# A fused block-sparse attention and feed-forward kernel: the second of four batches moves from dense masked attention to gathered key blocks

## The chip, the cores and the metric

The kernel runs on one core of a Trainium2 chip. The metric is the device time of one execution in microseconds (us). Matmuls run on TensorE (PE in the profile; PEld is its weight load), elementwise work on VectorE (DVE), ScalarE (ACT) and GpSimd (POOL). SyncE (SP) issues most of the DMA transfers; POOL issues those that cast or gather by an index. Each engine works through its own instructions in order.

## The reference

What is computed is BigBird-like attention (4 batches, 8 heads, 768 tokens, head size 64), whose output goes through a feed-forward layer with a squared ReLU. Tokens form 24 blocks of 32. A query block sees itself and its two neighbours, the first and the last block, and three blocks drawn for it; the first and the last query block see everything.

```python
mask = np.abs(blk_i - blk_j) <= 1
mask = mask | (blk_i == 0) | (blk_j == 0) | (blk_i == 23) | (blk_j == 23)
for qb in range(24):
    for kb in sampled_blocks[qb]:                      # 3 per query block
        mask[qb*32:(qb+1)*32, kb*32:(kb+1)*32] = True
attn = softmax(where(mask, q @ k.T / 8, -1e9)) @ v      # per batch and head
x = attn.transpose(0, 2, 1, 3).reshape(3072, 512)
out = square(maximum(x @ moe_w_in, 0)) @ moe_w_out      # 512 -> 2048 -> 512
```

## The kernel before

**Two kinds of attention.** Heads are handled in pairs: a batch has four units u (u = 0 to 3 is batch 0, 4 to 7 batch 1, and so on). Batches below the constant `SB` (before: 2) are *dense*. For each unit and each 256 queries, `scores` multiplies the queries with two 128-key chunks at a time; `exps` (line 360, ACT) takes the exponential of 128 x 1024 numbers; then the forbidden ones have to go. That is done in one of two ways. With `add` true, `scores` adds a large negative mask on TensorE (two further pairs of matmuls of `oh` and `R2`, before the exponential). With `add` false, `masks` (line 367, DVE) multiplies the exponentials by a 0/1 mask; batch-wide mask tiles for this are made once by `mask_tile` on TensorE and evacuated by `mask_evac`. `values` or `values_full` multiplies with V, and `normalize` divides by the sum.

Batches from `SB` on are *gathered*. Their queries are taken in six *visits* of two groups g of 64 queries each. A group needs 12 blocks of 32 keys at most: a window of four, the first and the last block, and 2 x 3 drawn ones. `k_gather` copies the drawn blocks of K inside SBUF (on DVE or POOL, with block numbers held in registers). V is written out to DRAM by `v_store` (`rows`), and read back by `v_window` (SP, fixed addresses) and `v_gather` (line 579, an indirect DMA from POOL with the index tile `idx`, or plain DMAs from SP with block numbers in registers). `s_scores`, `s_exps` (line 623), `s_masks` (line 630) and `s_values` (line 653) then work on 384 keys for a group and not on 768, except for the group g = 0, which is the first and the last query block. Loads of Q and K of such a batch are in pieces of 512 bytes (line 151), of a dense one in pieces of 1536 bytes (line 149). Its output is stored in another order, too.

**The block table.** `table_load`, `table_places`, `table_slots`, `table_spread`, `table_rows` and `table_masks` make from `sampled_blocks` the index tile, the masks `MKS` of the gathered batches, and the row `tab`, from which engines read block numbers into registers (`blocks_of`, line 561: a TENSOR_LOAD in the queue of DVE, POOL or SP). `table_slots` is one task of some twenty small DVE instructions; `table_rows` reads all block numbers that any engine wants, one group after the other.

**The feed-forward layer.** The tokens form 12 tiles of 256. For each, `hidden` has 16 parts of 8 matmuls, `relu` and `square` follow on ACT, DVE or POOL, and `output` has 8 parts of 8 matmuls. TensorE alternates between the attention of one batch and the feed-forward tiles of an earlier one. The weights are loaded as eight pieces by POOL (`w_load`). `loads_gate` makes SP wait for pieces 6 and 7 before it issues the loads of batch 1 and later ones.

**The order.** Nothing is scheduled at run time. Every piece of work is a numbered task, and the string `PROGRAM` lists all tasks in one order, each with the letter of its engine (P, V, A, G, S) and, for a task that takes PSUM, the place (X0 to X3). An engine's instructions stand in the order of its words. The four PSUM places and all SBUF buffers are handed on in this order, so a late task holds up those behind it on its engine and those that need its buffer.

```python
MASKED = ((256, 512), (512, 768), (0, 256))     # mask tiles that are made
attend(a, us[0] < HP and a[1] == 0)             # add the mask on TensorE: batch 0, first 256 queries
```

## Time and profile before

| | |
|---|---|
| median of 3 runs | 255.62 us (254.7 to 257.25) |
| the profiled execution | 258.88 us, span of its trace 257.1 us |
| granted TensorE clock | 1.00 |
| PE / PEld busy | 243.1 / 182.1 us |
| ACT / DVE / POOL busy | 183.6 / 171.3 / 98.8 us |
| DMA moved | 47.08 MB |

The span runs from the first to the last instruction of the trace. "Busy" is the time in which an engine had at least one instruction running; a matmul's row includes a tail in which the next one is already in. A row of groups reads: line, engine, operation, tiles written and read, shapes, count, then busy time, mean ns of one, and the idle time ahead of them with what ended it. A timeline row reads: start, length, engine, line, operation, tiles, shapes, count, and in brackets the idle time ahead of it.

### The profile page before, as it was taken

To read this page: it belongs to the slowest core of one execution; us is meant where nothing else is said; L and a number is where in the kernel's file an instruction comes from. 1 tells how busy PE (TensorE), PEld (TensorE's weight loads), DVE (VectorE), ACT (ScalarE), POOL (GpSimd) and SP (SyncE) were. 2 spreads that over 40 slices of the span, in tenths; PEclk is the share of its full clock that TensorE was granted. 3 is DMA by queue.
4 is the path that set the end of the run, shared out by engine and by line. 5 is a ranking of instruction groups with operands and counts; after the bars stand their busy time and mean duration, and the time that the engine had idled before them with its cause. 6 is when DMAs were issued, how large, how long until landed. Compare 5 with 4: busy or idle time off the path is not lost.

```text
span 257.1 us, 12061 instructions
## 1 busy us (share of the span) xinstructions
PE 243.1 (95%) x5265; PEld 182.1 (71%) x5265; DVE 171.3 (67%) x408; ACT 183.6 (71%) x217; POOL 98.8 (38%) x178
## 2 busy tenths in 40 slices
PE   7888999999999997998998999999999999999993
PEld 4667879678874677975864867866875677767683
DVE  7778988899889995969916756657536725730301
ACT  3899999998999797846783975675965286623640
POOL 3183247003316026198556314264357620412100
PEclk9999999999999999999999999999999999999999
DMA  6999989999999996999699779998474923044022
GB/s 200 374 250 207 206 205 155 270 202 252 250 281 179 197 202 153 340 229 154 188 243 202 194 174 167 251 214 199 129 206 95 189 40 60 5 121 148 23 86 83
DMA packets 64692, 47.08 MB, mean 183 GB/s; under 512 B 31567, under 2 KB 60624, under 8 KB 64640
## 3 DMA queue, kind: packets, MB, share of 16 engines
q1 hardware_dynamic: 58512, 37.82, 64.7%
q0 software_dynamic: 5440, 8.05, 16.8%
q8 instruction: 41, 0.67, 1.1%
q10 hardware_dynamic: 688, 0.46, 0.6%
q14 instruction: 11, 0.09, 0.1%
HBM read 35.51 MB, written 7.91 MB: 169 GB/s over the span
## 4 chain that ended last, share of the span: by engine, by line
PE 53%; DVE 5%; DVEq 1%; issue 1%; ACT 1%; ACTq 0%
PE X L203 49%; PE X L653 4%; DVE VB L123 1%; ACT pT L623 1%; DVEq L561 1%; DVE MKS L123 1%; DVE pT L630 1%; DVE r L709 0%; DVE KG L599 0%; DVE qc L123 0%; DVE XS L413 0%; DVE KG L593 0%; DVE XS L662 0%; DVEq L599 0%; DVE rs L410 0%
## 5 line engine op out<-in xcount | busy, mean ns | idle before, releaser
L203 PE MATMUL X<-xT,w_in_sb 64*128 64x256 bf16 x1536 | 100.8, 269 | 2.8 <-issue 1.5
L203 PE MATMUL X<-w_out_sb,g 64*128 64x512 bf16 (+3 forms) x960 | 95.2, 334 | 0.1
L203 PEld LDWEIGHTS <-w_in_sb 64*128 64x128 bf16 x1536 | 74.6, 94 | 16.0 <-issue 5.4
L360 ACT ACTIVATE pT<-X 128x1024 bf16<-128x1024 f32 x72 | 70.6, 1030 | 7.6 <-PE X L203 6.8
L623 ACT ACTIVATE pT<-X 128x768 bf16<-128x768 f32 (+1 forms) x56 | 41.6, 766 | 26.5 <-PE X L203 23.9
L203 PEld LDWEIGHTS <-g 64*128 64x128 bf16 x960 | 40.3, 94 | 26.3 <-PE X L203 0.4
L720 POOL TENSOR_TENSOR g<-r 128x1024 bf16<-128x1024 f32 (+1 forms) x20 | 31.6, 1587 | 64.4 <-ACT r L707 47.2
L707 ACT ACTIVATE r<-X 128x1024 f32<-128x1024 f32 x28 | 29.8, 1068 | 20.6 <-PE X L203 20.5
L709 DVE TENSOR_SCALAR r<-X 128x1024 f32<-128x1024 f32 x20 | 24.5, 1224 | 26.7 <-PE X L203 13.7
L367 DVE TENSOR_TENSOR pT<-pT,VG 128x1024 bf16<-128x1024 bf16 x60 | 40.9, 715 | 0.2
L718 ACT ACTIVATE g<-r 128x1024 bf16<-128x1024 f32 (+1 forms) x40 | 35.2, 899 | 2.7 <-DVE r L709 2.5
L203 PE MATMUL X<-QKT 64*128 64x256 bf16 (+1 forms) x384 | 31.6, 250 | 3.3 <-DVE XS L413 1.3
L630 DVE TENSOR_TENSOR pT<-pT,MKS 128x768 bf16<-128x768 bf16 (+1 forms) x48 | 27.6, 607 | 10.7 <-ACT pT L623 10.5
L203 PEld LDWEIGHTS <-QKT 64*128 64x128 bf16 x384 | 16.7, 95 | 9.5 <-issue 4.1
L579 POOL DMA_INDIRECT VG<-rows,idx x19 | 20.2, 1061 | 4.4 <-issue 2.6
L203 PEld LDWEIGHTS <-pT 64*128 64x128 bf16 x768 | 16.0, 94 | 1.9
L203 PE MATMUL X<-VB,pT 64*128 64x65 bf16 x768 | 17.1, 190 | 0.0
L203 PEld LDWEIGHTS <-KG 64*128 64x128 bf16 x528 | 13.8, 95 | 4.5 <-issue 0.2
L659 DVE RECIPROCAL ss<-X 128x8 f32<-128x8 f32 x12 | 2.5, 206 | 19.5 <-PE X L653 17.3
L653 PEld LDWEIGHTS <-pT 128*64 128x64 bf16 x624 | 11.9, 111 | 4.9 <-issue 3.7
L203 PE MATMUL X<-QKT,KG 64*128 64x64 bf16 x528 | 15.3, 190 | 0.1
L123 POOL CAST VB<-vs 128x768 bf16<-128x768 f32 x9 | 7.8, 869 | 16.5 <-DMA vs<-in_v_dram 16.4
(107 smaller groups left out, 210.3 us busy)
## 6 DMA issues: line engine op xcount, KB each, us to landing
vs<-in_v_dram SPq DMA_DIRECT2D x14, 384.0 KB
ks<-in_k_dram SPq DMA_DIRECT2D x13, 384.0 KB
qs<-in_q_dram SPq DMA_DIRECT2D x12, 384.0 KB
out_dram<-ys SPq DMA_DIRECT2D x9, 512.0 KB
VG<-rows SPq DMA_DIRECT2D x20, 132.0 KB
w_in_sb<-in_moe_w_in_dram POOLq DMA_DIRECT2D x4, 512.0 KB, 8.6
w_out_sb<-in_moe_w_out_dram POOLq DMA_DIRECT2D x4, 512.0 KB, 9.9
rows<-VB SPq DMA_DIRECT2D x2, 792.0 KB
```

What stands on the lines that cost most here:

```text
L123: (V if e == "DVE" else G).tensor_copy(out=out, in_=in_)
L203: last = nc.tensor.matmul(out(r ^ crossed), lhsT(r ^ crossed, rows), rhs(r ^ crossed, rows), skip_group_check=True, **kw)
L360: A.activation(out=pT[:, :, 0:n], in_=stile.pop(a)[:, :, 0:n], func=AF.Exp, scale=scale)
L367: V.tensor_tensor(out=pT, in0=pT, in1=m[:, None].broadcast_to([P, 2, len(cs), w]), op=AOP.mult)
L579: G.indirect_dma_start(out=to[0:RS * HB], out_offset=None, in_=pairs, in_offset=bass.IndirectOffsetOnAxis(ap=idx[0:RS * HB, g - 1:g], axis=0))
L623: A.activation(out=pT[:, :, 0:n], in_=stile.pop((u, v, gs))[:, :, 0:n], func=AF.Exp, scale=scale)
L630: V.tensor_tensor(out=pT, in0=pT, in1=m[:, None].broadcast_to([P, 2, n]), op=AOP.mult)
L653: nc.tensor.matmul(po[i * D:(i + 1) * D, h, a * VW:(a + 1) * VW], pts[g][:, h, c * D:(c + 1) * D], val, start=a == 0 and c == 0, stop=c == ...
L707: A.activation(out=to, in_=src, func=AF.Relu)
L709: V.tensor_scalar(out=to, in0=src, scalar1=0.0, scalar2=None, op0=AOP.max)
L718: A.activation(out=g, in_=r, func=AF.Square)
L720: (G if e == "POOL" else V).tensor_mul(out=g, in0=r, in1=r)
```

## The change

- `SB` becomes 1: batch 1 is gathered too. It drops 36 `scores`, `exps` and `masks`, its `values` and `normalize`; it gains a `v_store`, six visits, 11 `k_gather` and 11 `v_gather`, and its Q and K loads and its stores take the forms of the gathered batches.
- `MASKED` becomes empty, and `attend` adds the mask on TensorE for all of batch 0. No mask tile is made, and no `masks` task is left.
- `table_slots` is cut into `table_ids`, `table_dup`, `table_near`, `table_drawn` and `table_low`; its scratch moves from two `r` buffers to the two `ys` buffers, so `table_places` waits for `cast_v` of units 2 and 3, and one memset goes from DVE to POOL. The reading of block numbers becomes six tasks of its own, groups 1 to 3 and groups 4 to 11 for each of POOL, DVE and SP.
- `PROGRAM` is a new list. In it the first tasks are nearly the old ones; the eight weight pieces are issued by POOL in the order 1, 2, 0, 7, 6, 4, 3, 5 (before: 1, 2, 0, 3, 7, 6, 4, 5), the table is made from about the tenth hidden part on, and the visits of batch 1 begin after 36 hidden and 8 output parts, while the tiles of batch 0 are in work. POOL takes 31 of the `v_gather` (before 19), 15 `k_gather` (10), 30 `square` (20), 21 `cast_qk` (14); DVE 18 `k_gather` (12), 24 `relu` (20), 15 `cast_qk` (21). On SP the last store of the last tile is its largest part (256 KB).

```diff
-    SB, VR, KG_BUFS, VG_BUFS = 2, D + 2, 2, 3
+    SB, VR, KG_BUFS, VG_BUFS = 1, D + 2, 2, 3
...
-    MASKED = ((256, 512), (512, 768), (0, 256))
+    MASKED = ()
...
+    def table_scratch():
+        tmp = [YS[b_.at] for b_ in tb["tmp"]]
...
     def table_places(e):
...
-    def table_slots(e):
-        tmp = RT[tb["tmp"][0].at]
...
+        low[0] = table_scratch()[-1]
+        G.memset(low[0], 0.0)
+
+    def table_ids(e):
         V.tensor_copy(out=tab..., in_=sb_r...)
-        V.memset(low[0], 0.0)
         V.tensor_copy(out=ids[:, 6:SL], in_=sb_g...)
+        V.tensor_scalar(out=half, in0=lane, ...)
+        V.tensor_tensor(out=lane, in0=lane, in1=half, op=AOP.add)
+
+    def table_dup(e):        # is_equal, scalar_tensor_tensor, tensor_reduce, tensor_scalar
+    def table_near(e):       # subtract, is_ge, is_le
+    def table_drawn(e):      # is_equal, tensor_reduce, max, edges, mult by dup
+    def table_low(e):        # eight copies into low[0]
...
     def table_rows(e):
         V.tensor_scalar(out=idx, ...)
-        load_blocks("POOL")
-        load_blocks("DVE")
-        load_blocks("SP")
...
-    def load_blocks(e):
-        for g in wanted[e]:
+    def load_blocks(g0, g1, e):
+        for g in [g_ for g_ in wanted[e] if g0 <= g_ < g1]:
             if g not in held_at[e]:
                 held_at[e][g] = blocks_of(g, ENGINE[e])
...
-    p = T_(table_places)
-    tmp = tb["tmp"] = [Buf("r"), Buf("r")]
-    tb["slots"] = T_(table_slots, deps=[t, p], get=tmp)
+    tmp = tb["tmp"] = [Buf("ys"), Buf("ys")]
+    p = T_(table_places, get=tmp)
+    i_ = tb["ids"] = T_(table_ids, deps=[t, p])
+    for e_ in ("POOL", "DVE", "SP"):
+        T_(load_blocks, 0, 4, deps=[i_])
+        T_(load_blocks, 4, nb, deps=[i_])
+    d_ = T_(table_dup, deps=[i_])
+    n_ = T_(table_near, deps=[i_])
+    w_ = T_(table_drawn, deps=[d_, n_])
+    l_ = T_(table_low, deps=[w_])
...
+        if us[0] == 0:
+            p.deps += cv[2] + cv[3]
...
-            attend(a, us[0] < HP and a[1] == 0)
+            attend(a, True)
...
     PROGRAM = """
-        A29 G35 P4/3 V32 P30/0 P12/2 P14/3 P9/1 P5/1 V31 P33/1 V111 P36/3 ...
+        A36 P4/0 P37/1 P12/2 P14/3 G42 P9/0 P5/2 V39 V38 P40/3 P43/0 P0/2 ...
```

## The prediction

> **What bounds the kernel now.** I read the page first, then the stretches of the span between points where the kind of work changes, then single rows for prices.

> ```profile
> span 257.1 us, 12061 instructions
> PE 243.1 (95%) x5265; PEld 182.1 (71%) x5265; DVE 171.3 (67%) x408; ACT 183.6 (71%) x217; POOL 98.8 (38%) x178
> ```
> ```profile
> 0.00:27.75 27.75, 23.07 (x452) 17.55 (x454) 21.87 (x59) 22.06 (x26) 11.03 (x27) 1.00 1.04 254
> 27.75:91.55 63.80, 62.83 (x1412) 48.35 (x1407) 57.48 (x124) 59.94 (x68) 19.03 (x31) 1.00 1.09 218
> 91.55:148.74 57.19, 53.01 (x1199) 41.67 (x1194) 42.34 (x111) 40.66 (x49) 31.39 (x58) 1.00 0.96 212
> 148.74:225.71 76.97, 76.76 (x1654) 54.49 (x1653) 44.28 (x111) 49.78 (x61) 34.26 (x60) 1.00 0.67 144
> 225.71:257.10 31.39, 27.45 (x562) 20.01 (x560) 5.29 (x7) 11.13 (x16) 3.10 (x4) 1.00 0.29 94
> ```

> The columns are: stretch, its length, then busy time of PE, PEld, DVE, ACT, POOL, the granted clock, the share of the 16 DMA engines and GB/s. PE is the bound: it idles 14.0 us of 257.1, namely 4.7 in the opening, 1.0 until 91.55 us, 4.2 until 148.74, 0.2 until 225.71 and 3.9 at the end. The clock is 1.00 throughout. So this change can pay in two ways only: fewer matmuls, or some of those 14 us. Second, DMA stands at a share of 1.0 or more up to 91 us and falls to 0.67 and 0.29 later, so early traffic is dear and late traffic cheap. ACT (59.9 of 63.8) and DVE (57.5) are nearly full in the second stretch: that is the dense attention of two batches, with its exps and mask products.

> **The change part by part.** The sum is made on the profiled execution: span 257.1, 258.88 us in all. The runs shown have a median of 255.62, 3.3 below it; I apply the difference to the median.

> *Matmul work.* A row of a run of matmuls shows a tail after the last issue, so I price by the distance from one row's start to the next one's.

> ```profile
> 89.28 0.53 PE L203 MATMUL X<-VB,pT 64*128 64x65 bf16 x24
> 89.65 0.38 PE L203 MATMUL X<-QKT 64*128 64x256 bf16 x4
> 89.87 0.54 PE L203 MATMUL X<-VB,pT 64*128 64x65 bf16 x24
> ...
> 90.47 1.03 PE L203 MATMUL X<-w_out_sb,g 64*128 64x512 bf16 x8
> 91.33 0.38 PE L203 MATMUL X<-QKT 64*128 64x256 bf16 x4
> ```
> ```profile
> 7.14 0.27 PE L203 MATMUL X<-R,oh 64*128 64x256 bf16 x2
> 7.25 0.27 PE L203 MATMUL X<-QKT 64*128 64x256 bf16 x2
> ```
> ```profile
> 187.54 0.34 PE L203 MATMUL X<-QKT,KG 64*128 64x64 bf16 x12
> 187.72 0.60 PE L203 MATMUL X<-xT,w_in_sb 64*128 64x256 bf16 x8
> ```
> ```profile
> 207.13 0.95 PE L653 MATMUL X<-VG,pT 128*64 128x65 bf16 x48
> 208.02 1.05 PE L203 MATMUL X<-xT,w_in_sb 64*128 64x256 bf16 x16
> ```

> A dense `scores` of two key chunks costs 0.22 us, a half `values` 0.37, two masks added on PE 0.11, an `s_scores` of 12 matmuls 0.18, an `s_values` of 48 matmuls 0.89. Batch 1 loses 36 `scores` (7.9) and 24 half `values` (8.9). It gains 312 small score matmuls (26 x 0.18 = 4.7) and five `s_values` of 48 plus one of 72 (4.5 + 1.3 = 5.8). Batch 0 gains masks in 24 more `scores`, two pairs of matmuls at 0.11 each: 24 x 0.22 = 5.3; the nine mask tiles go, 9 x 0.11 = 1.0. Sum: -16.8 + 10.5 + 5.3 - 1.0 = **-2.0 us**. Everything in this line has its row, so I give it only +-0.5.

> *ACT, DVE and POOL.*

> ```profile
> L360 ACT ACTIVATE pT<-X 128x1024 bf16<-128x1024 f32 x72 | 70.6, 1030 | 7.6 <-PE X L203 6.8
> L367 DVE TENSOR_TENSOR pT<-pT,VG 128x1024 bf16<-128x1024 bf16 x60 | 40.9, 715 | 0.2
> L623 ACT ACTIVATE pT<-X 128x768 bf16<-128x768 f32 x48 | 38.0, 811 | 21.8 <-PE X L203 19.7 <-PE X L653 1.9
> L630 DVE TENSOR_TENSOR pT<-pT,MKS 128x768 bf16<-128x768 bf16 x40 | 23.3, 613 | 10.7 <-ACT pT L623 10.5
> L579 POOL DMA_INDIRECT VG<-rows,idx x19 | 20.2, 1061 | 4.4 <-issue 2.6
> ```

> ACT drops 36 exps (35.3 by the row's busy time) and takes 24 whole and 4 smaller ones, at most 28 x 0.81 = 22.7: 13 us less. DVE drops all 60 mask products (40.9) and takes 24 of about 0.61 or 28 at most (17): 24 us less, before some of the gather copies. POOL issues 31 gathers, not 19 (+12.7), and takes more casts, copies and squares. None of these bounds a stage, so the relief is worth only the PE waits that these two engines end: the 1.0 us up to 91.55 and what is not the table's in the 4.2 after it, 2.8. I take half of the 3.8, **-1.9**. Bounds: 0 (the same waits come back elsewhere) and -3.8 (all gone).

> *The block table.* Now it stands in one piece on DVE, with the reads of block numbers behind it.

> ```profile
> L561 DVEq TENSOR_LOAD <-tab x6: 857/992/1067, 93.8 to 99.2; - x6
> ```
> ```profile
> PE X L203 <- DVE XS L413: 1.0, 1, 1.0
> PE X L203 <- DMA xT<-XS: 0.4, 1, 0.4
> ```

> Six reads of 0.99 us hold DVE from 93.8 to 100.1; a `normalize` queued behind them makes PE wait 1.0 us, and an x tile is late by 0.4. In the change DVE reads two groups, later four, each set a task of its own, earlier, where the 40.9 us of mask products no longer stand in its queue. POOL reads its five right after the weight loads and SP two, so what is behind those (POOL's casts and SP's loads of batch 1) starts up to 5 us later than it might; its cover is that the gates are still shut. I credit the whole **-1.4**. Bounds: 0 and -1.4. The memset moved to POOL and the new scratch buffers cost nothing as long as `table_spread` has PE work around it; the order puts hidden tasks before and after it.

> *A second entry into gathered work.* In the new order PE meets the first visit of batch 1 after 36 `scores`, 8 full and 8 half `values`, 36 hidden parts and 8 output parts: at 0.44 (eight matmuls at 0.11 a pair), 0.74 (two halves), 0.37, 0.44 and 0.86 each (90.47 to 91.33) that is 47 us, with transposes and the table's matmuls about 50. The opening idles 4.7 us, and its matmul tails hide about as much again, so PE is there at about 60 us. The waits of that kind today are in the stretch 91.55 to 148.74; a second entry can cost nothing or the remaining 2.8 us again. I take **+0.6**, nearer to nothing, because ACT and DVE have room.

> *End.* In the new order the last store on SP is the 256 KB one, behind two smaller ones; today the last is 64 KB. I take **+0.6**, bounds 0 and 1.5: two SP issues of about 0.3 each and the longer transfer.

> ```profile
> 33.97 0.58 SPq L338 DMA_DIRECT2D scratch<-w_out_sb  x2
> ```

> (Two issues in 0.58 us: the price of one on SP. The row also shows when the gate opens now.)

> Sum: -2.0 - 1.9 - 1.4 + 0.6 + 0.6 = **-4.1 us**: span 253.0, on the median **251.5 us**.

> **The rivals.**

> *DMA falls behind (slower).* The gather's traffic is the one resource that grows where it is full.

> ```profile
> 20.00:35.00 15.00, 13.89 (x290) 11.43 (x288) 13.83 (x30) 14.72 (x18) 3.09 (x4) 1.00 1.20 200
> 35.00:40.00 5.00, 5.00 (x108) 4.14 (x106) 4.00 (x8) 4.67 (x7) 4.40 (x5) 1.00 0.66 177
> 100.00:105.00 5.00, 4.09 (x128) 4.09 (x129) 4.21 (x9) 3.74 (x5) 1.77 (x2) 1.00 0.62 198
> ```
> ```profile
> vs<-in_v_dram SPq DMA_DIRECT2D x14, 384.0 KB
> VG<-rows SPq DMA_DIRECT2D x20, 132.0 KB
> rows<-VB SPq DMA_DIRECT2D x2, 792.0 KB
> VG<-rows SPq DMA_DIRECT2D x16, 66.0 KB
> VG<-rows SPq DMA_DIRECT2D x18, 33.0 KB
> ```

> For two batches SP moves 1.6 MB out and 4.3 MB back, and POOL's 19 gathers of 96 rows x 2112 bytes 3.9 MB: 4.9 MB per batch. At the 212 GB/s of the stretch table that is 23 us of DMA, all before batch 2's first `s_values`, which the new order reaches about when the old one does (101 against 104 us of work ahead of it). Against it: the gate now waits for the fourth and fifth weight piece, not the sixth (one piece of 0.5 MB at 200 GB/s is 2.6 us: about 4 us earlier), and the stretches at 0.66 and 0.62 leave 3.6 us. So 15 us must come from shares above those seen, or from slack. A share up to 1.20 occurred, which is why this is a rival and not the forecast. If half of the 15 us is not absorbed, PE stands 7.5 us before batch 1's or batch 2's first values, and the relief and the table's credit are lost too: -2.0 + 0.6 + 0.6 + 7.5 = +6.7, **262.3 us**. It decides from about 5 us of such standing on.

> *The waits only move.* The waits of the third stretch are those of feeding visits, not of dense masks: the relief is 0 and the second entry costs 2.8. -2.0 - 1.4 + 2.8 + 0.6 = 0.0: **255.6**. For it: ACT and DVE are at 71 to 74% in that stretch and PE still idles. Against it: up to 91.55 us both are near full.

> *POOL slows DVE.* The trace has DVE instructions that stretch beside POOL's copies and gathers:

> ```profile
> 114.06 1.97 DVE L630 TENSOR_TENSOR pT<-pT,MKS 128x384 bf16<-128x384 bf16 x1
> 118.63 0.55 DVE L123 CAST VB<-vs 128x768 bf16<-128x768 f32 x1
> 120.29 2.62 DVE L123 CAST VB<-vs 128x768 bf16<-128x768 f32 x1
> ```

> The same cast takes 0.55 or 2.62 us. Batch 1 brings 12 gathers and 5 sets of POOL copies more; if one in four stretches a DVE instruction that PE waits for, by the 2 us seen, that is 17 x 2 / 4 = 8.5 us, less the relief that it eats: -4.1 + 8.5 = +4.4, **260.0**; at one in eight it is back at no change. Against it: in the fourth stretch POOL does such work beside DVE and PE idles 0.2 us. [...] I go by the stretch.

> **How the numbers follow.** The forecast 0.50, DMA behind 0.22, waits only move 0.18, POOL slows DVE 0.10. Within the forecast the terms' bounds give -2.5 - 3.8 - 1.4 = -7.7, 248, to -1.5 + 2.8 + 1.5 = +2.8, 258; its own range is 248 to 256. The matmul tails can hide as much again as the visible idle in the third stretch, so I let the low end go to 246; the high end takes in the DMA case, 263. A measurement of this kernel tells about 1%, 2.6 us, from no change. Faster: 0.46 of the forecast and 0.04 of the moved waits, 0.50. Same: 0.03 of the forecast, 0.13 of the moved waits, 0.06 of POOL: 0.22. Slower: the rest, 0.28.

> **What would show it.** Right: no TENSOR_LOAD run of 6 us on DVE, no mask product on L367, PE idle under 1.5 us between 60 and 120 us, DVE near 147 and ACT near 155 us or below. DMA behind: PE or DVE rows that wait for `QKT`, `VG` or `vs` between 60 and 120 us and a share at 1.1 or more there. Moved waits: PE idle of 4 us or more between 60 and 120 us that names ACT or DVE. POOL: DVE casts and mask products with means well over 0.55 and 0.61 us. The forecast is wrong if PE's idle time before 150 us is not below today's 9.9 us.

## The result and the profile after

The change makes the kernel slower: 279.22 us (276.33 to 280.64) against 256.44 us (254.7 to 258.93), a ratio of 1.088, 95% interval 1.073 to 1.102. The forecast was 251.5. Ratios here compare the quicker executions alone, because some executions of one and the same kernel take a few per cent longer; medians count all of them. The profiled execution is the longest of the four, 280.64 us, and its span is 278.9. First the page: the sizes and busy times of the engines, then the DMA queues.

```profile
span 278.9 us, 12152 instructions
PE 248.3 (89%) x5247; PEld 178.1 (64%) x5247; DVE 165.6 (59%) x394; ACT 155.5 (56%) x192; POOL 148.6 (53%) x257
q1 hardware_dynamic: 64880, 40.32, 69.1%
q0 software_dynamic: 6208, 10.48, 18.9%
q8 instruction: 41, 0.67, 1.1%
```

The same queues on the page of before:

```profile
q1 hardware_dynamic: 58512, 37.82, 64.7%
q0 software_dynamic: 5440, 8.05, 16.8%
q8 instruction: 41, 0.67, 1.1%
```

The columns are packets, MB and the time of the packets as a share of 16 engines' span. ACT and DVE have become lighter, as planned, and PE is still the bound, but it idles 30.6 us, not 14.0. The last line will matter: a DMA queue of its own moves 41 packets, 0.67 MB in all, that no line of the kernel asks for.

Stretches cut where the kind of work changes show the place (columns as before: stretch, length, busy PE, PEld, DVE, ACT, POOL, clock, DMA share, GB/s):

```profile
27.75:60.00 32.25, 30.60 (x625) 24.54 (x623) 13.49 (x45) 28.23 (x36) 7.42 (x15) 1.00 1.20 237
60.00:74.00 14.00, 13.80 (x288) 9.09 (x286) 5.73 (x21) 8.95 (x12) 7.95 (x16) 1.00 1.04 213
74.00:112.00 38.00, 29.22 (x646) 19.25 (x642) 22.56 (x58) 18.41 (x24) 21.44 (x51) 0.91 1.17 222
112.00:150.00 38.00, 34.04 (x800) 25.31 (x796) 27.04 (x71) 24.92 (x31) 28.28 (x44) 1.00 0.95 205
```

From 74 to 112 us, where the first four visits of batch 1 are computed, PE stands 8.8 us, the clock is 0.91 and the DMA share is 1.17. DVE, ACT and POOL are idle for 41 to 52% of it, so none of them is full. The chain of work that ended last (start, length, what) has these pieces of 1 us and more in which PE stands, from 20 to 106 us, and they name neither data nor an engine:

```profile
42.24 1.35 issue
80.90 1.74 issue
88.43 1.50 issue
95.85 1.25 issue
101.85 3.26 issue
```

"issue" means that the wait has no releaser in the trace. The timeline of PE shows where such a wait falls:

```profile
100.93 0.92 PE L666 MATMUL X<-VG,pT 128*64 128x65 bf16 x45
105.11 0.32 PE L666 MATMUL X<-VG,pT 128*64 128x65 bf16 x3 [3.26 <-issue]
```

| packet | PE passes position 193 | packet runs | PE stands at the next position 193 |
|---|---|---|---|
| 10 | 75.8 us | 79.31 to 81.04 | 80.5 to 82.6 |
| 11 | 82.6 | 87.06 to 88.33 | 88.2 to 89.9 |
| 12 | 89.9 | 94.47 to 95.47 | 95.7 to 97.1 |
| 13 | 97.1 | 102.43 to 103.70 | 101.7 to 105.1 |
| 30 | 207.51 | 207.54 to 208.68 | not for it (215.6) |

When DMA is quiet (last row, a share of 0.11 from 207 to 209 us) the packet runs 0.03 us after PE has passed; the 0.9 us that PE idles at 215.6 us name gathered keys (`DVE KG`). In the other rows (a share of 1.20 from 75.8 to 104 us) it starts 3.5 to 5.3 us later, runs 1.0 to 1.7 us, and PE goes on 1.4 to 1.6 us after its end. What of this lasts longer than PE needs for its 256 instructions shows here as a stall. In the four visits PE needs 4.6 to 5.7 us for a block; in the kernel before, in its dense stretch from 53 to 99 us, it needs 4.7 to 6.8 us, and the packets start 1.5 to 3.4 us late. So it is the longer wait of the packets, far more than denser instructions, that makes the stalls of the change. Two more stretches show what follows a long stall:

```profile
18.00:24.00 6.00, 5.92 (x120) 4.83 (x118) 3.32 (x14) 3.29 (x4) 5.77 (x17) 0.72 1.22 198
104.00:112.00 8.00, 6.76 (x85) 4.50 (x87) 4.47 (x8) 1.62 (x2) 2.35 (x3) 0.57 1.04 178
```

From 19.1 us on for 3.4 us and from 104.4 us on for 6.8 us the granted clock is 0.50 ("half clock" below; the 12 matmuls of an `s_scores` take 0.34 us at 109 us, 0.18 at 112): behind a wait of 2.2 us for a cast on POOL that ends at 17.6 us, and with the stall of 3.26 us.

Taking the time from the start of one weight load or matmul to the start of the next, the profiled run of after has 13.5 us of stalls at position 193 where before has 1.1 (0.5 and 0.6), and 10.2 us of half clock, worth up to 5.1 us by estimate (half of its length). The other gaps over half a microsecond between the first 15 us and the end sum to 11 us against 7. 12.4 and at most 5.1 and 4 are about the 21.8 us by which the span has grown; the matmul work gives 1.8 back.

### The profile page after: what moved, and what is told of

Read it like the earlier page. It is cut to its first block, busy times and chain, and to the rows that moved or that the text cites. A ratio compares the mean times of both kernels' runs of the same rounds, so it can differ in the third digit from the quotient of the medians.

```text
span 278.9 us, 12152 instructions
## 1 busy us (share of the span) xinstructions
PE 248.3 (89%) x5247; PEld 178.1 (64%) x5247; DVE 165.6 (59%) x394; ACT 155.5 (56%) x192; POOL 148.6 (53%) x257
## 3 DMA queue, kind: packets, MB, share of 16 engines
q1 hardware_dynamic: 64880, 40.32, 69.1%
q0 software_dynamic: 6208, 10.48, 18.9%
## 4 chain that ended last, share of the span: by engine, by line
PE 66%; DMA 10%; issue 9%; DVE 6%; SPq 4%; POOL 1%; ACT 1%; DVEq 0%; POOLq 0%; ACTq 0%
PE X L203 58%; PE X L666 6%; DMA VG<-rows 4%; DVE KG L612 3%; DMA qs<-in_q_dram 3%; DMA vs<-in_v_dram 2%; PE X L398 2%; DMA VG<-rows,idx 2%; SPq L679 1%; SPq L169 1%; SPq L565 1%; SPq L151 1%; POOL qc L123 1%; SPq L569 1%; ACT pT L360 1%
## 5 line engine op out<-in xcount | busy, mean ns | idle before, releaser
L203 PE MATMUL X<-xT,w_in_sb 64*128 64x256 bf16 x1536 | 104.1, 274 | 2.6 <-issue 1.2
L203 PE MATMUL X<-w_out_sb,g 64*128 64x512 bf16 (+3 forms) x960 | 94.4, 334 | 1.9 <-issue 1.7
L636 ACT ACTIVATE pT<-X 128x768 bf16<-128x768 f32 (+1 forms) x84 | 61.9, 765 | 59.5 <-PE X L203 59.0
L203 PEld LDWEIGHTS <-w_in_sb 64*128 64x128 bf16 x1536 | 71.4, 95 | 23.1 <-PE X L203 7.2
L733 POOL TENSOR_TENSOR g<-r 128x1024 bf16<-128x1024 f32 (+1 forms) x30 | 50.8, 1701 | 36.0 <-DVE r L722 26.0
L203 PEld LDWEIGHTS <-g 64*128 64x128 bf16 x960 | 39.0, 94 | 30.4 <-issue 2.0
L643 DVE TENSOR_TENSOR pT<-pT,MKS 128x768 bf16<-128x768 bf16 (+1 forms) x72 | 44.6, 656 | 9.1 <-ACT pT L636 8.9
L360 ACT ACTIVATE pT<-X 128x1024 bf16<-128x1024 f32 x36 | 35.0, 1032 | 4.9 <-PE X L203 3.8
L592 POOL DMA_INDIRECT VG<-rows,idx x31 | 30.5, 983 | 11.7 <-issue 4.2
L720 ACT ACTIVATE r<-X 128x1024 f32<-128x1024 f32 x24 | 25.8, 1078 | 17.1 <-PE X L203 16.8
L731 ACT ACTIVATE g<-r 128x1024 bf16<-128x1024 f32 (+1 forms) x30 | 25.8, 871 | 15.1 <-DVE r L722 15.0
L612 DVE COPY KG<-QKT 128x64 int32 x108 | 27.7, 331 | 0.0
L666 PE MATMUL X<-VG,pT 128*64 128x65 bf16 x792 | 19.7, 197 | 8.9 <-issue 4.8
L203 PEld LDWEIGHTS <-KG 64*128 64x128 bf16 x792 | 19.8, 96 | 12.2 <-POOL g L733 3.1
L666 PEld LDWEIGHTS <-pT 128*64 128x64 bf16 x936 | 18.0, 111 | 14.5 <-issue 12.4
L203 PE MATMUL X<-QKT,KG 64*128 64x64 bf16 x792 | 22.3, 192 | 5.5 <-issue 2.7
L203 PE MATMUL X<-QKT 64*128 64x256 bf16 (+1 forms) x288 | 22.2, 234 | 1.2 <-DVE QKT L123 0.4
L123 POOL CAST qc<-ks 128x384 bf16<-128x384 f32 x14 | 6.7, 510 | 29.3 <-PE X L203 18.9
L612 POOL COPY KG<-QKT 128x64 int32 x90 | 21.4, 283 | 0.0
L203 PE MATMUL X<-R,oh 64*128 64x256 bf16 x144 | 18.0, 275 | 0.0
## 6 DMA issues: line engine op xcount, KB each, us to landing
vs<-in_v_dram SPq DMA_DIRECT2D x14, 384.0 KB
ks<-in_k_dram SPq DMA_DIRECT2D x13, 384.0 KB
qs<-in_q_dram SPq DMA_DIRECT2D x12, 384.0 KB
VG<-rows SPq DMA_DIRECT2D x30, 132.0 KB
rows<-VB SPq DMA_DIRECT2D x3, 792.0 KB
```

The costliest lines, as they stand in the source:

```text
L123: (V if e == "DVE" else G).tensor_copy(out=out, in_=in_)
L203: last = nc.tensor.matmul(out(r ^ crossed), lhsT(r ^ crossed, rows), rhs(r ^ crossed, rows), skip_group_check=True, **kw)
L360: A.activation(out=pT[:, :, 0:n], in_=stile.pop(a)[:, :, 0:n], func=AF.Exp, scale=scale)
L592: G.indirect_dma_start(out=to[0:RS * HB], out_offset=None, in_=pairs, in_offset=bass.IndirectOffsetOnAxis(ap=idx[0:RS * HB, g - 1:g], axis=0))
L612: eng.tensor_copy(out=rows[:, :, :, r_ * w:(r_ + 1) * w], in_=src[:, :, :, bass.ds(at[r_] * w, w)])
L636: A.activation(out=pT[:, :, 0:n], in_=stile.pop((u, v, gs))[:, :, 0:n], func=AF.Exp, scale=scale)
```

## The experiments

Theory 1: PE's instructions, fetched in blocks by DMA, come late because the change fills the DMA engines and its gathered visits use instructions fast. Rivals: late data; POOL and DVE slowing each other; the feeding chain of the visits. Each comparison has its own runs of the kernel before, on the same chip; their medians differ from chip to chip, 256.3 to 261.6 us, so differences count for more than times. "Stalls" are gaps of PE of 0.5 us and more at position 193, from start to start as above, summed over the profiled run.

**Moving the stream.** `shift_after`: `N_WARM` 14 becomes 30, 64 instructions more at the start.

> The kernel after, with 16 warm-up pairs more at the very start: 64 more TensorE instructions (weight loads and matmuls) ahead of everything, nothing else changed. Theory 1 (TensorE stands because its own instructions, fetched 256 at a time by DMA, come late): the stalls that wait for nothing lie again 193 to 195 instructions past a multiple of 256, now counted with the 64 more, so each one falls 64 instructions earlier in the work; the ones over 1 us are again four or more between 75 and 112 us; time 276 to 283 us. Rival (these stalls belong to certain visits, for data or buffers that the profile doesn't name): they stay with the same matmuls and so lie at 1 to 3 past a multiple of 256.

281.82 us. The chain of work:

```profile
83.87 1.63 issue
91.47 2.50 issue
101.65 0.91 issue
146.78 2.49 issue
```

Counted anew these stalls begin at 3265, 3521, 3777 and 5569, all at position 193 again, 64 instructions earlier in the work. The tie to the count is shown; the rival falls. Stalls of 0.5 us or more make 9.4 us in this single run, and of those over 1 us only three, not four, lie between 75 and 112 us.

**More instructions alone, in the kernel before.**

```diff
-            pair(lambda h: ps[:, h, j * w:(j + 1) * w], ..., lambda h, rows: QK[i][rows, 0, qsl], start=j == 0, ...)
+            for z in range(0, w, D):
+                pair(lambda h: ps[:, h, j * w + z:j * w + z + D], ...,
+                     lambda h, rows: QK[i][rows, 0, q0 + z:q0 + z + D], start=j == 0 and z == 0, ...)
```

> The kernel before, with every dense score matmul of 256 columns cut into four of 64 columns: same result, same loads and stores, some 2000 more TensorE instructions (8 more blocks of 256) between about 20 and 92 us. The gathered scores already run at 29 ns per pair of 64 columns, against 27 for a quarter of a 256-column pair, so the matmul work itself grows by about 1 us. Theory 1: a fetch takes 2 to 3.5 us in the queue plus 2.5 us, 4.6 to 6 us, and 256 instructions now last about 4 us in dense attention: stalls without a wait at the 256-instruction positions, and 8 to 20 us more, 264 to 276 us. Rival (data late by DMA, or DVE and POOL in each other's way): neither changes, 255 to 259 us, no such stalls.

279.65 us against 261.56, ratio 1.072 (1.063 to 1.081): 18 us from 1728 instructions, without a byte of data more. PE's waits (waited for, total us, times, longest):

```profile
PE X L203 <- issue: 19.4, 17, 2.5
PE X L399 <- issue: 1.6, 1, 1.6
```

The stalls sum to 22.5 us in the profiled run, each ending 1.2 to 1.7 us behind a packet of queue q8; at most of them PE had needed only 3.3 to 4.3 us for its 256 instructions. The increase lies within the 8 to 20 us expected (the time itself above the 276, on a chip where before is 5 us slower), and it is nearly as much as the whole change costs. So density alone can bring such stalls too.

**More traffic alone, in the kernel before.** `traffic_before`: at ten places of the order, `dma_start` from 256 rows of 2 KB of `moe_w_in` to a DRAM tile of its own, on SP.

> The kernel before, with ten copies of 512 KB from DRAM to DRAM (rows of 2 KB, 5.2 MB in all, about what the change adds) that nothing waits for, issued by SP between about 60 and 115 us. Theory 1: stalls without a wait at the 256-instruction positions in that stretch, three or more of 0.5 us and over, besides waits for late data; time up by 4 to 10 us, 260 to 267 us. Rival (only data comes late): the added stalls of TensorE name a DMA or an engine fed by one, and none over 0.5 us is without a wait.

277.4 us, ratio 1.066 (1.054 to 1.079). More than expected, and not by theory 1. PE's waits:

```profile
PE X L208 <- DMA xT<-XS: 4.3, 2, 3.8
PE X L208 <- DMA QKT<-qc: 4.0, 1, 4.0
PE X L658 <- DMA VG<-rows: 2.7, 1, 2.7
PE X L208 <- issue: 1.6, 4, 0.9
```

Only one stall at position 193 (1.3 us): the transposes and V rows come late first, and each of three waits of 3.0 to 4.2 us comes with 6.8 us of half clock. SP issued the copies between 78 and 141 us. The first long wait, up to 102.9 us, falls into the dense stretch, the other two, up to 125.4 and 147.7 us, into the gathered visits, which begin at 115 us here. PE's packets wait up to 5.4 us in the queue in this run too, but mostly unseen: of the four that wait 3.9 to 4.2 us between 78 and 99 us only one shows as a stall, with 5.2 us of PE's work for its block; two had 6.8 and 7.0 us, and one a wait for data of 4.0 us beside it. Why data come first in these visits, and instructions in those of the changed kernel, is not shown.

**Less traffic, in the kernel after.** `load` returns without a transfer, for batch 2 (`lessload`) or for batches 2 and 3 (`noload`).

> The kernel after without the loads of Q, K and V of batch 2 (4.7 MB, issued between about 60 and 115 us; the buffers keep earlier data, so batch 2's output is not the reference's). Every instruction of the engines and every wait on them stays. Theory 1: the stalls without a wait between 75 and 106 us (7.8 us) go, and with them the 6.8 us of half clock behind the longest: 266 to 271 us; those at 157 and 169 us stay. Rival (DVE and POOL in each other's way, or the visits' own chain of copies, scores, masks): the time stays within 3 us of 279.

274.05 us, ratio 1.043 (1.028 to 1.059). The stretch that lost most:

```profile
74.00:112.00 38.00, 35.60 (x828) 24.28 (x826) 31.70 (x68) 25.37 (x33) 26.89 (x47) 1.00 0.61 140
```

At a share of 0.61 PE idles 2.4 us, not 8.8, and no stall of 0.5 us is left at position 193; with all other work unchanged, the stalls of this stretch come from full DMA engines. From 112 us on the run loses as the changed kernel does. Its time is above the 266 to 271 us expected, but so is before on this chip: it is 12.5 us over before, where the change costs 22.8, and a gain of some 10 us is what theory 1 said.

> The changed kernel as it is, as the yardstick for the others of this comparison. 276 to 286 us, 20 to 24 us over before. The stalls of TensorE at the 256-instruction positions are there again between 75 and 110 us.

279.55 us against 256.34, ratio 1.083 (1.071 to 1.095): the yardstick stands; its stalls are 11.9 us.

> The changed kernel without any load of Q, K and V of batches 2 and 3 (24 loads, 9.4 MB; the buffers keep earlier data, so the output of these batches is not the reference's). All instructions of TensorE, ScalarE, VectorE and POOL stay. Theory 1 and late data together (the DMA engines are full, and both TensorE's instructions and its data come late): most of the 23 us goes, 259 to 264 us where before has 256. Rival (the rest is VectorE and POOL making the gathered keys and masks, which no load touches): 268 us or more.

> The kernel before without any load of Q, K and V of batches 2 and 3, the same as in noload_after, as its control. If DMA holds the kernel before up nowhere by more than the 1.1 us of its two stalls at 256-instruction positions: 0 to 3 us below before.

`noload_after` 267.62, ratio 1.027 (1.016 to 1.038); `noload_before` 261.51, ratio 1.011 (1.006 to 1.017). 6.1 us remain between them where 23 were: three quarters of the loss go when these transfers go, and the stalls fall to 1.9 and 0 us. Both expectations missed in their times: 267.62 is over the 264 and just short of the rival's line, and the control is not faster but 1% slower. Before ran 259.45 here, though, so the rest is about 8 us over it (7 by the ratio), at the edge of the 3 to 8 expected and well under the rival's 12. That before gains nothing without 9.4 MB gives no sign that DMA holds it up; why it loses is open.

**Fewer instructions, in the kernel after.**

```diff
-                pair(lambda h: ps[:, h, at:at + D], ..., lambda h, rows: queries(rows), ...)
-                at += D
+                if v and g == gs[1]:
+                    continue
+                n = 2 * D if v else D
+                pair(lambda h: ps[:, h, at:at + n], ..., lambda h, rows: both(rows) if v else queries(rows), ...)
+                at += n
...
-                        nc.tensor.matmul(po[i * D:(i + 1) * D, h, a * VW:(a + 1) * VW], ...)
+                        nc.tensor.matmul(po[i * D:(i + 1) * D, h, a * VW:a * VW + wide], ...)   # two heads, every other a
```

> The changed kernel; in the gathered visits but the first of each batch, s_scores multiplies the keys of the first group alone with the queries of both (6 matmuls of 128 columns, not 12 of 64), and s_values takes the columns of two heads at once (24 matmuls of 132 columns, not 48 of 65): half the TensorE instructions for about the same column work, so the output of batches 1 to 3 is not the reference's. Loads, gathers, copies, exponentials and their waits are the same. About 190 instructions fewer per visit, 2900 in all or 11 blocks of 256, of some 1000 to 1300 between two stalls' worth of visits. Theory 1 (instructions come late): the stalls at the 256-instruction positions between 75 and 110 us fall to under a third, time 6 to 12 us below the yardstick. Rival (late data, DVE and POOL): within 2 us of the yardstick, or the visits' PE waits name data instead.

The edit leaves out 1440 instructions, 96 a visit and six packets of q8: half of what was expected. 271.9 us, 7.7 below the yardstick, ratio to before 1.052 (1.043 to 1.061). Of it 1.4 us is plain matmul time: 15 `s_values` at 0.813 where they had 0.882, 60 `s_scores` at 0.168 where they had 0.174. The stalls fall from 11.9 to 2.0 us. What takes their place:

```profile
PE X L203 <- DMA xT<-XS: 3.2, 2, 2.6
PE X L676 <- DMA VG<-rows: 2.5, 1, 2.5
PE X L203 <- DMA QKT<-qc: 1.8, 3, 1.0
```

With its instructions in time, PE meets the late data that stood right behind them.

> Both at once: half the TensorE instructions in the gathered visits, as in fewer_after, and no loads of batches 2 and 3. If instructions and data come late for one reason, full DMA engines, the two savings overlap: no more than 3 us below noload_after. If they are separate, they add: 6 us or more below it.

261.87 us, ratio 1.008 (1.003 to 1.013), 0.4 us over `noload_before`: with both, the whole loss against this control is gone. The two savings neither overlap as fully as one cause would have it (5.8 us below `noload_after`, 1.4 of it plain matmul time) nor add in full. Since `noload_after` has only 1.9 us of stalls left, part of the 5.8 us must come from something else that fewer instructions relieve; what, is open.

**POOL and DVE.** `nocopies_after`: `for r_ in range(0 if known else RS)` in `k_gather`.

> The changed kernel; k_gather copies the drawn key blocks only the first time that each of its buffers is filled, later visits keep them: 174 of the 198 small copies are left out (about 24 us of VectorE, 19 us of POOL), so the output is not the reference's. No transfer changes. Theory 1 and late data: 0 to 3 us below the yardstick (the DVE KG waits of TensorE, 2 to 3 us, go). Rival (POOL and VectorE, slowing each other in these copies, hold the visits up): 6 us or more below it.

280.18 us, the yardstick's time; ratio 1.075 (1.064 to 1.087) where the yardstick has 1.083. The groups, and PE's waits:

```profile
L613 POOL COPY KG<-QKT 128x64 int32 x12 | 2.6, 261 | 0.0
L613 DVE COPY KG<-QKT 128x64 int32 x12 | 1.4, 186 | 0.0
```
```profile
PE X L667 <- issue: 7.2, 5, 3.4
PE X L203 <- issue: 5.1, 6, 1.5
```

These copies took 49 us of two engines in the changed kernel (the rows stand below) and take 4 here; no gain that is clear of noise comes of it, and the stalls are still there (12.3 us). The rival's 6 us or more falls.

**Two parts of the change alone, in the kernel before.** `before_masks` calls `attend(a, us[0] < HP)`; `before_table` has `table_slots` in five tasks and `load_blocks` in tasks of their own.

> The kernel before with one part of the change alone: batch 0's masks are all added on TensorE and its 24 products on VectorE are gone; the mask tiles stay, since dense batch 1 needs them. By the prediction's prices 24 times 0.22 = 5.3 us of matmuls more, less at most 1 us of TensorE waits that ScalarE or VectorE ended: 4 to 6 us over before. Theory 1 adds 200 instructions to a stretch with fetches of 4.6 to 6 us per 256: up to 2 us more.

> The kernel before with another part of the change alone: the block table in small tasks, and the block numbers read by POOL, VectorE and SyncE in tasks of their own (two groups on VectorE at the old place, the other four behind the third gather copy). The prediction credited 1.4 us for this: 0 to 1.4 us below before. Theory 1 says nothing of it.

`before_masks` 261.97 against 256.34, ratio 1.023 (1.017 to 1.030): 5.6 us more, no stall. `before_table` 257.08, ratio 1.002 (0.995 to 1.009): no gain to be seen.

**Fewer instructions with the result kept.** In `hidden` and `output` four matmuls over all 128 rows take the place of eight on 64-row halves.

```diff
+        i, j = divmod(part, n)
+        for kc in range(KM):
+            nc.tensor.matmul(htile[T, f][:, i, j * w:(j + 1) * w], w_in_sb[:, kc, ...], xT[b, c0][:, kc], ...)
```

> The changed kernel, with the feed-forward layer's matmuls over all 128 rows in place of pairs of 64-row halves: hidden parts have 4 matmuls of 256 columns, not 8 on half the rows each, output parts 4 of 512 columns, not 8. Same result, same transfers, same column work (a pair of halves runs in the time of one full matmul: 0.11 and 0.216 us), 2300 TensorE instructions fewer, 9 blocks of 256. Theory 1 (TensorE's instructions come late behind full DMA engines): fewer and shorter stalls at the 256-instruction positions, under 6 us in all where the changed kernel has 12 to 16, and 4 to 9 us below the changed kernel, 17 to 20 us over before at most. Late data alone: no change beyond 2 us. A third way (the load of 128-row weights isn't hidden, as in values_full, where 0.84 us stand against 0.72 for the halves): TensorE's own work grows, by up to 16% of the feed-forward layer's 167 us.

> The same edit in the kernel before: 2300 TensorE instructions fewer at the same column work. Its stalls at 256-instruction positions are 1.1 us, so by theory 1 0 to 2 us below before: the version that could beat both. If the weight load of full rows isn't hidden: slower, by up to 26 us.

`full_before` 274.73 against 260.73, ratio 1.063 (1.056 to 1.070): the third way. A matmul by itself has its price (0.109 and 0.216 us from one to the next), but a part takes 0.54 us, not 0.44, and 0.97, not 0.86: the change between kinds of work now shows (a dense `scores` takes 0.32 us, not 0.22). Both edits leave out some 2500 instructions, not 2300. `full_after` 272.52, ratio 1.056 (1.047 to 1.066), 7 us *below* the changed kernel in spite of this, within the 4 to 9 that theory 1 expected, and 2.2 below its control, though the two intervals overlap. Its page and `full_before`'s:

```profile
span 270.5 us, 9657 instructions
PE 256.6 (95%) x3999; PEld 173.9 (64%) x3999; DVE 163.7 (61%) x394; ACT 155.8 (58%) x192; POOL 149.1 (55%) x257
```
```profile
span 272.9 us, 9565 instructions
PE 261.1 (96%) x4017; PEld 170.8 (63%) x4017; DVE 169.9 (62%) x408; ACT 185.8 (68%) x217; POOL 99.8 (37%) x178
```

Here, with 2500 instructions fewer and PE slower, the change costs nothing more; a gain of the 2 us that its matmul count says is not clear of noise.

> full_after with each of its feed-forward matmuls cut into two of half the columns: the same result, rows, column work and transfers, the slower matmul work of full_after, but the 2300 instructions are back (some 10400 in all). Theory 1 (late instructions): the stalls at the 256-instruction positions are back, 6 us or more in all, and against its control fullsplit_before it is 4 us or more slower. Late data alone: such stalls stay below 5 us, and it is no slower than fullsplit_before, as full_after is 2 us faster than full_before. Where a second weight load shows, both kernels pay it alike.

> The same edit on full_before, as the control: 0 to 8 us over full_before for weight loads that show, stalls at the 256-instruction positions under 3 us.

The edit: each of these matmuls in two halves of its columns. `fullsplit_after` 280.35, ratio 1.096 (1.085 to 1.107); `fullsplit_before` 276.45, ratio 1.076 (1.066 to 1.087). A part costs 0.01 us more in both, as expected. The 2500 instructions turn the change from 2.2 us faster to 3.9 us slower, 6 us at one matmul work and one traffic. But the stalls are 3.3 us, not 6, and `full_after` has 2.4: only 0.9 of the 6 us are stalls. The rest lies in waits beside them (1.9 us for `VG` where `full_after` has 0.4, 2.9 where it has 2.1 for the cast at 18 us) and in the clock, which was granted at 0.988 in the mean where `full_after` has 0.999, by estimate some 3 us of the span. So this pair does not tell late instructions from late data.

So it is shown that PE's instructions come late between 74 and 112 us of the changed kernel, that the DMA load brings this about (`lessload_after`), and that it costs several microseconds (6 us in `fewer_after` beyond the matmul time). That full DMA engines always reach the instructions first is not shown; in `traffic_before` they reached the data first. How the 23 us divide between late instructions, late data right behind them and the halved clock is not settled to better than some 6 us: where one is taken away, the next fills part of the gap. No version beat the kernel before.

## Why the prediction was wrong

**Matmul work, -2.0: right.** Counted at the median pace of each form of matmul in its trace, without the warm-up, PE's work takes 225.9 us before and 224.1 after, -1.8; the masks alone were priced at 5.3 and measured 5.6; `full_after` lies 2.2 below its control.

**Relief of ACT, DVE, -1.9: failed.** ACT came out at 155.5, as forecast; DVE at 165.6, not 147, and PE still waits 3.6 us for it (`ss`, `KG`).

```profile
L643 DVE TENSOR_TENSOR pT<-pT,MKS 128x768 bf16<-128x768 bf16 x60 | 40.6, 710 | 9.1 <-ACT pT L636 8.9
L612 DVE COPY KG<-QKT 128x64 int32 x108 | 27.7, 331 | 0.0
L612 POOL COPY KG<-QKT 128x64 int32 x90 | 21.4, 283 | 0.0
```

One product takes 0.71 us where 0.61 was shown, but all products together take the 44.6 us that the prediction's numbers give. The excess is the gather copies: on DVE they are busy for 27.7 us, before for 9.7. The prediction named them ("before some of the gather copies") and gave them no term. Before, such a copy took 205 ns on DVE and 242 on POOL. That DVE's rows grow longer is what the POOL rival said would happen; no run here shows that POOL is the cause. The rival's price of 2 us per piece was wrong: `nocopies_after` gains nothing clear of noise.

**Block table, -1.4: not seen.** The part alone measured 0.7 us slower; -1.4 is the edge of its interval. In any case it is small.

**Second entry, +0.6: this step failed most.** Between 74 and 112 us PE idles 8.8 us, before 1.7, and 6.8 us of half clock cost up to 3.4 more: some 10 us. Until 150 us PE idles 20.3 us, where the prediction called itself wrong from 9.9 on. The step asked whether DVE and ACT can feed the visits, and but for 0.8 us (`KG`) they are not what PE waits for there. It left out PE's own supply of instructions, which queue q8 on the page of before shows, and with it the wait that full DMA engines put on that queue: 1.5 to 3.4 us per packet before (from 53 to 99 us), 3.5 to 5.3 in the visits.

**End, +0.6: about right** (from PE's last matmul to the end of the span it is 4.5 us, before 3.8).

**The rival of DMA falling behind had the right resource.** The forecast put this term at nothing, although its own working left 15 us that only shares above those seen, or slack, could take in. The rival's test, a share of 1.1 or more with PE waiting between 60 and 120 us, came true for the share and not for the names: `QKT` and `VG` were not what PE waited for there. Its size was wrong twice. The page's queues took 64.7 and 16.8% of 257.1 us before, 210 us, and take 69.1 and 18.9% of 278.9 after, 245: 36 us more, not 23, though the bytes grew by the 4.9 MB that were forecast. V traffic was priced; batch 1's Q and K loads in pieces of 512 bytes were named in the change and not priced (512- and 1536-byte packets of the first queue together take 67.0 us of the 16 engines, before 57.9). And what a late transfer costs was put at 7.5 us, as one wait for data, when it also holds up instructions and brings half clock.

In the kernel before, stalls at position 193 made 1.1 us, so little of the wait for instructions showed there; after, they made 13.5. The prediction had no term for it.

## What to carry to other kernels

Where DMA engines are full, count TensorE's instructions as traffic that is due: in these kernels every 256 of them need a fetch, which waited 0.03 us at a DMA share of 0.11 and 3.5 to 5.3 us at 1.20, and 1728 instructions more, in small matmuls, came with 22.5 us of stalls (`split_before`). A wait without a releaser in the middle of a task was the sign (3.26 us between the 45th and 46th matmul of an `s_values`); count the instructions up to it. Before adding traffic to a kernel that lives at a DMA share above 1, ask what comes late first, and put a price on every transfer whose form changes, not only on the new ones.

## What the hardware showed unexpectedly

- A packet ran only about one block ahead of its use: the earliest of the 82 in the two kernels' traces started 1.6 us before PE passed position 193 (packet 37 of before), one with DMA at rest 0.03 us after it, those of the four visits 3.5 to 5.3 us after it, and a late one stopped PE exactly one block on. From the end of the packet to PE's next instruction it was 1.4 us at the two stalls of before, 1.4 to 1.6 us at those of after and 1.2 to 1.7 us in `split_before`.
- Half clock came in stretches of 3.4 or 6.8 us behind waits of 2.2 us and more; some of 2.3 to 2.7 us brought it and others of that length did not (2.5 us for the cast on POOL came with a clock of 0.95 up to 20 us and 0.96 up to 40 in `fewer_after`, and with 1.000 over the whole span in `noload_after`), and single stalls of 2.1 us and less left the clock alone (in `split_before` four waits of 0.6 to 0.7 us, almost in a row, brought 3.4 us of it at 143.8 us).
- A matmul over all 128 rows has the price of a pair on halves (0.109 us at 256 columns), but a part of four of them costs 0.105 us more when other work comes between, and so does a `scores` or an `s_scores` beside it (0.107 us more).
